# Softmax reciprocals spread over partitions by transfers inside SBUF, and normalization two pairs sooner, in an attention and feed-forward kernel

## The chip, the cores and the metric

One core of a Trainium2 chip runs the whole program. The metric is the device time of one execution in microseconds (us), the median of several runs. PE is the TensorE matmul, PEld its weight load, DVE VectorE, ACT ScalarE, POOL GpSimd, SP SyncE, which here only issues transfers (DMAs).

## What is computed

There are 2 batches of 12 heads, 448 tokens each, 64 numbers per head. After the attention come two feed-forward blocks, the second gated and with an RMS norm.

```
scores = cap * tanh(q @ k.T / sqrt(64) / cap)
attn   = exp(scores - max) / (sum + 1e-9);  x = attn @ v          # 896 x 768 over all heads
h = x @ w_in;   x = (h * sigmoid(1.702 h)) @ w_out                # 768 -> 2048 -> 768
xn = x / rms(x) * g;  out = (silu(xn @ w_gate) * (xn @ w_val)) @ w_out2   # 768 -> 1536 -> 768
```

The change concerns `attn / sum`: each head's output is multiplied by the reciprocal of its row sum, one number per token, which has to stand on all 64 partitions of the head.

## The kernel before, in words

**Pairs.** Attention works on 12 pairs of heads (`NPR` = 12). Pair p has its 2 x 64 output numbers on the 128 partitions and 448 tokens along the free dimension. The loop runs p from 0 to 12; iteration p makes the scores, tanh and exp of pair p and the output products, row sums and reciprocal of pair p-1. The instructions of every engine run in the order in which the program writes them (`manual_schedule`), so each engine is a queue: an instruction that waits holds all that is behind it. SP's and ACT's DMA issues stand in the same queues.

**One iteration from p = 3 on, by engine.** PE: `scores(p, 1)`, `scores(p, 2)` (L246), `scores_last(p)` (L255), `outputs(p-1)` (L294), `sums(p-1)` (L332), `scores(p+1, 0)`. ACT: four tanh (L275) and two exp (L278: `pa`, then `pb`). DVE: perhaps a normalization, `split_kq(p+2)` (L226, L227), `add_two(p)` (L314, needs the exp of `pa`), `copy_out(p-1)` (L306), the reciprocal of `sums(p-1)` (L337). POOL: `add_third(p)` (L319), which DVE does for the last pair. `sums(p-1)` needs the result of `add_third(p-1)`.

**PSUM.** The pool `ps_v` has two banks and three users in an iteration, in this order: `scores_last(p)`, `outputs(p-1)`, `sums(p-1)`. So `outputs(p)` gets the bank that `sums(p-1)` used and cannot start until the reciprocal of pair p-1 has read it. Likewise `scores_last(p+1)` waits for `copy_out(p-1)`.

**Reciprocals.** The reciprocal `rs` is a tile of 128 x 224: four groups of 32 equal rows, for two heads e and two halves j of the tokens. For pairs 0 to 8, `keep_recips` (L342) writes four rows to DRAM, and `spread` (L347), two iterations later, reads them back over all partitions into `r`. For pairs 9 to 11, four small matmuls (`spread_product`, L353) with a selection matrix `sel` do it, into PSUM.

**Normalization** of a pair is `norm_mul` (L368, L371 or L375, DVE), `norm_hi` (L380 on DVE for p < 8, L382 on ACT from p = 8 on) and `norm_lo` (L387, DVE). Pairs 0 to 4 are normalized five iterations after their scores (`norm(p-5)`), pairs 5 to 7 at the end of an iteration four later, pairs 8 to 10 in iteration 12, pair 11 inside the first feed-forward.

**Weights** come as units of 768 KB. A unit is loaded into one of three `raw` buffers (L112), decoded by ACT and DVE (`scale`, `shift`, `top`, `low`, then `high_part` on ACT, L156, and `low_part` on DVE, L161) and used by three matmuls for each block (`group`, L567 to L569). Units 0 to 2 are decoded partly during attention, by a `plan` of places: (4, "b") is place b of iteration 4, for example. Units 2 and 3 are finished while the first two columns of the feed-forward run. A column is 18 matmuls: two columns over tokens 0 to 383, four over tokens 384 to 895, and so on; the third column is the first that reads pair 11.

Of the kernel before, what the change touches and what calls it, by code (L numbers as in the profile page):

```python
# [17 lines left out]
def attn_moe_kernel(  # L18
# [36 lines left out]
    tiny = keep.tile([128, 1], F32, name="tiny")  # L55
    blk = keep.tile([128, 128], F32, name="blk")
    ones = keep.tile([128, 128], F32R, name="ones")
    sel = keep.tile([128, 64], F32, name="sel")
    gcol = keep.tile([128, KD], F32, name="gcol")
    xA = [keep.tile([128, KD, NT], F32R, name=f"x{i}") for i in range(2)]  # L60
    CUT = 384
# [45 lines left out]
    def load_to(u):  # L107
        while nload[0] <= min(u, len(units) - 1):
            w = nload[0]
            t = pools['raw'].tile([128, 6, 128, 2], U32, tag="raw", name="raw")  # L110
            for b0, n, s in units[w]:
                nc.sync.dma_start(out=t[:, b0:b0 + n].rearrange("p k f t -> p k (f t)"), in_=s)  # L112
            raw_t[w] = t
            nload[0] += 1
# [27 lines left out]
    def low(w):  # L142
        d, lo, hi = dec_t[w]
        nc.vector.scalar_tensor_tensor(  # L144
            out=d, in0=lo, scalar=29, in1=d, op0=ALU.logical_shift_right, op1=ALU.bitwise_or
        )
        if w != 2:
            load_to(w + 3)

    def high_part(w):  # L150
# [24 lines left out]
    def attention():  # L175
        with ExitStack() as actx:
# [9 lines left out]
            def constants():  # L186
                for e in range(2):
                    nc.gpsimd.memset(blk[half[e], half[e]], 1.0)
                    nc.gpsimd.memset(blk[half[e], half[1 - e]], 0.0)
                nc.gpsimd.memset(sel, 0.0)  # L190
                for n in range(4):
                    nc.gpsimd.memset(sel[32 * n:32 * n + 1], 1.0)

            xs, raws, vs, pa, pb, zt, nr, ts_ = {}, {}, {}, {}, {}, {}, {}, {}

# [85 lines left out]
                return pa[p][:, c] if c < 2 else pb[p][:, 0:2]  # L281

            opened = {}
            late = {}

            def outputs(p, cs=range(NC + 1)):
                if 0 in cs:
                    opened[p] = ps_v.tile([128, 512], F32, tag="v", name="v")
                ps = opened[p]
                for c in cs:  # L290
                    for n in range(4):
                        e, d0 = n // 2, n % 2 * 32
                        w = vs[p][:, e * NC + c if c < NC else 2 * NC + e]
                        nc.tensor.matmul(  # L294
                            out=ps[32 * n:32 * n + 32, 0:S], lhsT=w[:, d0:d0 + 32],
                            rhs=probs(p, c)[:, e] if c < NC else pb[p][:, 2],
                            start=(c == 0), stop=(c == NC), skip_group_check=True,
                        )
# [22 lines left out]
            def sums(p):  # L321
                ps = ps_v.tile([128, 512], F32, tag="v", name="v")
                streams = [ts_[p], *([pb[p][:, 0:2]] if p < THREE else []), None]
                for n, some in enumerate(streams):
                    for e in range(2):
                        for j in range(2):
                            if some is None:
                                w, t = blk[:, 64 * e:64 * e + 32], pb[p][:, 2]
                            else:
                                w, t = f(ones)[:, 0:32], some[:, e]  # L330
                            r0 = 64 * e + 32 * j
                            nc.tensor.matmul(  # L332
                                out=ps[r0:r0 + 32, 0:SH], lhsT=w, rhs=t[:, j * SH:(j + 1) * SH],
                                start=(n == 0), stop=some is None, skip_group_check=True,
                            )
                nr[p] = zrp.tile([128, SH], F32, tag="rs", name="rs", bufs=4)
                nc.vector.reciprocal(out=nr[p], in_=ps[:, 0:SH])  # L337

            def keep_recips(p):
                rs = nr[p]  # L340
                nr[p] = dram.tile([4, SH], F32, tag="recs", name="recs", bufs=3)
                nc.sync.dma_start(out=nr[p], in_=rs[0:128:32])  # L342

            def spread(p):
                d = nr[p].rearrange("(e j) n -> e (j n)", j=2)
                nr[p] = zrp.tile([128, S], F32, tag="r", name="r", bufs=3)
                nc.sync.dma_start(out=nr[p], in_=d.unsqueeze(1).to_broadcast([2, 64, S]))  # L347

            def spread_product(p, banks):
                for j in range(2):  # L350
                    for e in range(2):
                        quarter = slice(64 * e + 32 * j, 64 * e + 32 * j + 32)
                        nc.tensor.matmul(  # L353
                            out=banks[j][half[e]], lhsT=sel[quarter], rhs=nr[p][quarter],
                            start=True, stop=True, skip_group_check=True,
                        )
                nr[p] = banks

            def spread_late(p):
                if not late:  # L360
                    ps_s.tile([128, 2, 512], F32, tag="s", name="none")
                late[p] = ps_s.tile([128, 2, 512], F32, tag="s", name="late")[:, :, 0:SH]
                spread_product(p, [late[p][:, j] for j in range(2)])

            def norm_mul(p):
                r = nr.pop(p)
                if p < NPR - 3:
                    nc.vector.tensor_tensor(out=zt[p], in0=zt[p], in1=r, op=ALU.mult)  # L368
                elif p < NPR - 1:
                    zz = zt[p].rearrange("p (j n) -> p j n", j=2)  # L370
                    nc.vector.tensor_tensor(out=zz, in0=zz, in1=late[p], op=ALU.mult)  # L371
                else:
                    for j in range(2):
                        zz = zt[p][:, j * SH:(j + 1) * SH]
                        nc.vector.tensor_tensor(out=zz, in0=zz, in1=r[j], op=ALU.mult)  # L375

            def norm_hi(p):
                b, pp = divmod(p, NP)
# [12 lines left out]
            def norm(p):  # L391
                for step in (norm_mul, norm_hi, norm_lo):
                    step(p)
# [33 lines left out]
            scale_by_cap()  # L427

            EARLY = 3

            def products(p):
                outputs(p, range(NC + 1) if p else (2, NC))
                if p + 1 >= NPR - 1:
                    spread_late(p - 1)
                decode(p + 1, "a")
                if p < NPR - 1:
                    copy_out(p, "D")
                sums(p)

            for p in range(NPR + 1):  # L440
                load_kq(p + 3)
                load_v(p + 2)
                if 0 < p < 3:
                    load_to(p)
                if p == 0:
                    scores(0, 0)
                    tanh(0, 0)
# [28 lines left out]
                        exp(pa[p])  # L476
                    exp(pb[p])
                if 3 <= p < NPR:
                    spread(p - 3)
                if 5 <= p < NPR - 2:  # L480
                    norm(p - 5)
                decode(p, "b")
                if p + 2 < NPR:
                    split_kq(p + 2)
# [1 line left out]
                if p < NPR:  # L486
                    add_two(p)
                    decode(p, "d")
                if p == NPR:
                    norm_mul(p - 4)  # L490
                if p >= EARLY:
                    products(p - 1)
                    scores(p + 1, 0)
                if 1 <= p < NPR - 2:
                    keep_recips(p - 1)
                if p < NPR:
                    add_third(p)
                if p == NPR - 1:
                    norm_mul(p - 2)
                if NPR - 3 <= p < NPR:  # L500
                    norm(p - 4)
                if p == NPR:
                    copy_out(p - 1, "A")
                    some = (p - 3, p - 2, p - 4)
                    norm_mul(p - 2)
                    for step in (norm_hi, norm_lo):
                        for q_ in some:
                            step(q_)
            return spread_product, norm_mul, norm_hi, norm_lo

    def rest(spread_product, norm_mul, norm_hi, norm_lo):
        with ExitStack() as fctx:
            pools["ring1"] = fctx.enter_context(tc.tile_pool(name="ring1", bufs=3, reuse_waits="tile"))
            bigp = fctx.enter_context(tc.tile_pool(name="big", bufs=1, reuse_waits="tile"))
# [3 lines left out]
            def bank():  # L518
                return ps.tile([128, 512], F32, tag="b", name="b")
# [63 lines left out]
            def later(*fns):  # L583
                at(1, *[("D", True, fn) for fn in fns])
# [27 lines left out]
            for c in range(NC1):  # L612
# [9 lines left out]
                if c == 0:  # L622
# [2 lines left out]
                        + [(op, 3) for op in DVE_OPS] + [(op, 4) for op in ACT_OPS] + slots[0]  # L625
                    )
                    slots[0] = []
                if c == 0:
                    q3 = NPR - 1
                for n, (i, b) in enumerate(order):  # L630
                    last = ()
                    if c == 0 and n == 0:
                        later(lambda: spread_product(q3, [bank()[:, 0:B * S // 4] for _ in range(2)]))
                        later(lambda: norm_mul(q3), lambda: norm_hi(q3), lambda: run(shift, 2), lambda: norm_lo(q3))
                        last = (
                            lambda: [run(*some) for some in first], lambda: load_to(5), load_g,
                        )
                    ffn1(gA, u0 + i, i, b, slots[n], last)
# [247 lines left out]
```

## Time and profile before

| | |
|---|---|
| median of 3 runs | 589.24 us (588.69 to 590.09) |
| the profiled execution: its time, its span | 589.35 us, 587.5 us |
| PE, PEld, DVE, ACT, POOL busy | 99%, 83%, 71%, 47%, 10% |
| granted TensorE clock | 1.00 in nearly all of the span |
| start of the first feed-forward column | 91.19 us |

The span runs from the first to the last profiled instruction; the remaining 1.85 us lie around it. Times of rows count from the start of the span. A row "x16" of the timeline is 16 merged instructions. In brackets stands the idle time of the engine before it and what ended that.

### The profile page before, as it was taken

How to read it: one execution, taken by the hardware profiler on the slowest of the kernel's cores; microseconds unless marked ns; L12 is line 12 of the kernel's file. 1: busy time of each engine (PE TensorE's matmuls, PEld its weight loads, DVE VectorE, ACT ScalarE, POOL GpSimd, SP SyncE). 2: the span in 40 equal slices, each digit the busy share in tenths (PEclk: the TensorE clock that was granted, in tenths of full speed). 3: DMA queues.
4: the chain of work that ended last, by engine and by line, in shares of the span. 5: the costliest groups of instructions: out<-in, count | busy, mean ns of one | idle time of the engine just before them, and what ended most of it. 6: DMA issues, size and time to landing. Idle time of an engine off the chain costs nothing.

```text
span 587.5 us, 8371 instructions
## 1 busy us (share of the span) xinstructions
PE 581.6 (99%) x3390; PEld 487.6 (83%) x3390; DVE 418.5 (71%) x542; ACT 276.6 (47%) x371; POOL 59.2 (10%) x49
## 2 busy tenths in 40 slices
PE   9999999999999999999999999999999999999997
PEld 4455547898988889898999898989898998989887
DVE  4899987966736336566687999883587894678742
ACT  6999984754433335454444434443233331233300
POOL 0022320000000000000213012100122100222000
PEclk9999999999999999999999999999999999999999
DMA  8734510742443313333333333343133352133022
GB/s 285 268 125 149 158 50 6 211 162 101 152 126 107 108 54 108 108 107 108 108 108 108 108 108 113 121 152 99 54 109 109 108 189 80 55 107 108 1 89 98
DMA packets 55168, 67.91 MB, mean 116 GB/s; under 512 B 2998, under 2 KB 49882, under 8 KB 55130
## 3 DMA queue, kind: packets, MB, share of 16 engines
q1 hardware_dynamic: 54986, 67.15, 35.0%
q8 instruction: 26, 0.43, 0.3%
q10 hardware_dynamic: 144, 0.23, 0.1%
q14 instruction: 12, 0.10, 0.1%
HBM read 64.59 MB, written 2.78 MB: 115 GB/s over the span
## 4 chain that ended last, share of the span: by engine, by line
PE 97%; ACT 2%; issue 0%; DVE 0%
PE b L569 28%; PE b L568 28%; PE b L567 28%; PE v L294 6%; PE s L246 3%; PE v L332 2%; PE v L255 1%; ACT pa L275 1%; ACT pb L278 0%; ACT pb L275 0%; PE v L414 0%; ACT pa L278 0%; PE late L353 0%; PE b L709 0%; PE v L412 0%
## 5 line engine op out<-in xcount | busy, mean ns | idle before, releaser
L569 PE MATMUL b<-x,ring 128*128 128x384 f32 (+1 forms) x480 | 173.9, 362 | 0.0
L567 PE MATMUL b<-x,ring 128*128 128x384 f32 (+1 forms) x480 | 173.8, 362 | 0.0
L568 PE MATMUL b<-x,ring 128*128 128x384 f32 (+1 forms) x480 | 173.8, 362 | 0.0
L567 PEld LDWEIGHTS b<-x,ring 128*128 128x128 f32 x480 | 90.1, 188 | 10.2 <-DVE x L387 0.7
L568 PEld LDWEIGHTS b<-x,ring 128*128 128x128 f32 x480 | 90.1, 188 | 9.5
L569 PEld LDWEIGHTS b<-x,ring 128*128 128x128 f32 x480 | 90.1, 188 | 9.4
L161 DVE TENSOR_TENSOR ring<-dec,ring 128x768 fp32r<-128x768 f32 x68 | 77.2, 1136 | 28.1 <-ACT ring L156 28.1
L156 ACT ACTIVATE ring<-dec 128x768 fp32r<-128x768 f32 x67 | 56.1, 837 | 31.5 <-DVE dec L144 26.2
L569 PE MATMUL b<-g,ring 128*128 128x512 f32 (+1 forms) x192 | 69.7, 363 | 0.0
L568 PE MATMUL b<-g,ring 128*128 128x512 f32 (+1 forms) x192 | 69.6, 363 | 0.0
L567 PE MATMUL b<-g,ring 128*128 128x512 f32 (+1 forms) x192 | 69.5, 362 | 0.0
L144 DVE SCALAR_TENSOR_TENSOR dec<-raw,dec 128x768 uint32<-128x768 uint32 x68 | 66.9, 983 | 1.2
L138 DVE SCALAR_TENSOR_TENSOR dec<-raw,dec 128x768 uint32<-128x768 uint32 x68 | 64.8, 952 | 1.0
L130 ACT ACTIVATE dec<-raw 128x768 f32<-128x768 f32 x66 | 59.2, 897 | 5.0 <-issue 2.5
L569 PE MATMUL b<-uA,ring 128*128 128x512 f32 (+1 forms) x144 | 52.1, 362 | 0.0
L568 PE MATMUL b<-uA,ring 128*128 128x512 f32 (+1 forms) x144 | 52.1, 362 | 0.0
L567 PE MATMUL b<-uA,ring 128*128 128x512 f32 (+1 forms) x144 | 52.1, 362 | 0.0
L599 DVE TENSOR_TENSOR g<-gg,g 128x384 fp32r<-128x384 f32 (+1 forms) x32 | 20.0, 624 | 40.6 <-ACT g L596 40.6
L741 POOL TENSOR_TENSOR a<-a,gg 128x512 f32<-128x512 f32 (+1 forms) x18 | 29.2, 1622 | 187.1 <-DVE gg L734 179.9
L744 ACT ACTIVATE uA<-a 128x512 fp32r<-128x512 f32 (+1 forms) x24 | 13.9, 580 | 70.4 <-POOL a L741 52.1
L134 DVE TENSOR_SCALAR dec<-dec 128x768 uint32<-128x768 uint32 x68 | 39.4, 579 | 0.0
L568 PEld LDWEIGHTS b<-g,ring 128*128 128x128 f32 x192 | 36.0, 188 | 3.9
(93 smaller groups left out, 670.9 us busy)
## 6 DMA issues: line engine op xcount, KB each, us to landing
raw<-in_moe_w_out SPq DMA_DIRECT2D x20, 768.0 KB
raw<-in_moe_w_in SPq DMA_DIRECT2D x16, 768.0 KB
raw<-in_moe_w_gate SPq DMA_DIRECT2D x12, 768.0 KB
raw<-in_moe_w_val SPq DMA_DIRECT2D x12, 768.0 KB
raw<-in_moe_w_out SPq DMA_DIRECT2D x8, 512.0 KB
v<-in_v SPq DMA_DIRECT2D x12, 256.0 KB
kq<-in_k SPq DMA_DIRECT2D x11, 256.0 KB
kq<-in_q SPq DMA_DIRECT2D x11, 224.0 KB
```

Of the source, the lines that this page charges most:

```text
L130: nc.scalar.activation(out=f(d), in_=f(hi), func=AF.Copy, scale=2.0 ** -112)
L134: nc.vector.tensor_scalar(out=d, in0=d, scalar1=3, scalar2=None, op0=ALU.logical_shift_left)
L138: nc.vector.scalar_tensor_tensor(out=d, in0=hi, scalar=0x80000000, in1=d, op0=ALU.bitwise_and, op1=ALU.bitwise_or)
L144: nc.vector.scalar_tensor_tensor(out=d, in0=lo, scalar=29, in1=d, op0=ALU.logical_shift_right, op1=ALU.bitwise_or)
L156: nc.scalar.activation(out=t[:, 0], in_=f(dec_t[w][0]), func=AF.Copy)
L161: nc.vector.tensor_tensor(out=t[:, 1], in0=f(d), in1=f(t[:, 0]), op=ALU.subtract)
L294: nc.tensor.matmul(out=ps[32 * n:32 * n + 32, 0:S], lhsT=w[:, d0:d0 + 32], rhs=probs(p, c)[:, e] if c < NC else pb[p][:, 2], start=(c == 0 ...
L567: nc.tensor.matmul(out=wide(o, b), lhsT=w0, rhs=x0, start=first, stop=False)
L568: nc.tensor.matmul(out=wide(o, b), lhsT=w0, rhs=x1, start=False, stop=False)
L569: nc.tensor.matmul(out=wide(o, b), lhsT=w1, rhs=x0, start=False, stop=last)
L599: nc.vector.tensor_tensor(out=gA[1].at(i, hb), in0=gg[0], in1=f(gA[0].at(i, hb)), op=ALU.subtract)
L741: eng.tensor_tensor(out=t[0], in0=t[0], in1=t[1], op=ALU.mult)
```

## The change

- All 12 pairs use the same `spread(p)`: four DMAs from SBUF to SBUF, each of 64 rows of 224 numbers, from one half j of `rs` to every second partition of `r`. The sums are put at other partitions for that (`r0`). The DMAs are issued from SP directly behind the reciprocal, in the iteration after the pair's scores; for the last pair, two of the four are issued from ACT.
- `keep_recips`, `spread_product`, `spread_late`, the matrix `sel` and its five memsets go.
- `norm(p-3)` takes the place of `norm(p-5)`, from iteration 3 to 11; pair 9 is normalized at the end of iteration 11, pair 10 in iteration 12, pair 11 in the feed-forward with `shift(2)` and `top(2)` ahead of it.
- `outputs(11)` writes to a bank of `ps_s` in place of `ps_v`.
- Weight units 1 to 4 are loaded at the starts of iterations 3, 5, 7 and 9; before, units 1 to 3 were issued in iteration 1 and unit 4 after `low(1)` in iteration 7.

```diff
-        if w != 2:
+        if w > 2:
             load_to(w + 3)
...
             def outputs(p, cs=range(NC + 1)):
                 if 0 in cs:
-                    opened[p] = ps_v.tile([128, 512], F32, tag="v", name="v")
+                    if p < NPR - 1:
+                        opened[p] = ps_v.tile([128, 512], F32, tag="v", name="v")
+                    else:
+                        ps_s.tile([128, 2, 512], F32, tag="s", name="none")
+                        opened[p] = ps_s.tile([128, 2, 512], F32, tag="s", name="s")[:, 0]
...
-                            r0 = 64 * e + 32 * j
+                            r0 = 64 * j + 32 * e
...
+            def spread(p):
                 rs = nr[p]
                 nr[p] = zrp.tile([128, S], F32, tag="r", name="r", bufs=3)
-                nc.sync.dma_start(out=nr[p], in_=d.unsqueeze(1).to_broadcast([2, 64, S]))
...
                 for j in range(2):
+                    for i in range(2):
+                        eng = nc.scalar if j and p == NPR - 1 else nc.sync
+                        eng.dma_start(out=nr[p][i:128:2, j * SH:(j + 1) * SH], in_=rs[64 * j:64 * j + 64])
...
             def norm_mul(p):
+                nc.vector.tensor_tensor(out=zt[p], in0=zt[p], in1=nr.pop(p), op=ALU.mult)
...
+            RAW = {3: 1, 5: 2, 7: 3, 9: 4}
             def products(p):
                 outputs(p, range(NC + 1) if p else (2, NC))
-                if p + 1 >= NPR - 1:
-                    spread_late(p - 1)
...
-                if 0 < p < 3:
-                    load_to(p)
+                if p in RAW:
+                    load_to(RAW[p])
...
                 if 3 <= p < NPR:
-                    spread(p - 3)
-                if 5 <= p < NPR - 2:
-                    norm(p - 5)
+                    norm(p - 3)
                 decode(p, "b")
...
-                if p == NPR:
-                    norm_mul(p - 4)
                 if p >= EARLY:
                     products(p - 1)
                     scores(p + 1, 0)
-                if 1 <= p < NPR - 2:
-                    keep_recips(p - 1)
+                if p >= 1:
+                    spread(p - 1)
                 if p < NPR:
                     add_third(p)
                 if p == NPR - 1:
-                    norm_mul(p - 2)
-                if NPR - 3 <= p < NPR:
-                    norm(p - 4)
+                    norm(p - 2)
                 if p == NPR:
                     copy_out(p - 1, "A")
-                    some = (p - 3, p - 2, p - 4)
-                    norm_mul(p - 2)
-                    for step in (norm_hi, norm_lo):
-                        for q_ in some:
-                            step(q_)
+                    norm(p - 2)
...
-                        later(lambda: spread_product(q3, [bank()[:, 0:B * S // 4] for _ in range(2)]))
-                        later(lambda: norm_mul(q3), lambda: norm_hi(q3), lambda: run(shift, 2), lambda: norm_lo(q3))
+                        later(lambda: run(shift, 2), lambda: run(top, 2), *norm_last)
```

## Rows read from the trace of the kernel before

**Rows 1.** The page's first part: busy us, share, instructions of each engine.

```profile
PE 581.6 (99%) x3390; PEld 487.6 (83%) x3390; DVE 418.5 (71%) x542; ACT 276.6 (47%) x371; POOL 59.2 (10%) x49
```

**Rows 2.** Stretches: length, busy us of PE, PEld, DVE, ACT, POOL; clock, DMA share, GB/s.

```profile
34.00:61.00 27.00, 27.00 (x296) 13.99 (x295) 26.00 (x33) 24.98 (x25) 7.86 (x5) 1.00 0.49 151
...
76.00:81.00 5.00, 5.00 (x62) 2.77 (x58) 4.40 (x6) 4.64 (x5) 1.50 (x1) 1.00 0.13 48
...
102.00:331.00 229.00, 229.00 (x1135) 205.36 (x1134) 147.63 (x192) 107.28 (x166) 11.68 (x10) 1.00 0.37 118
```

**Rows 3.** Timeline: start, length, engine, line; reciprocals and output products.

```profile
32.25 1.55 DVE L337 RECIPROCAL rs<-v 128x224 f32<-128x224 f32 x1
...
33.90 1.71 PE L294 MATMUL v<-pa,v 128*32 128x448 f32 x16 [0.31 <-ACT pa L275]
...
39.11 1.56 DVE L337 RECIPROCAL rs<-v 128x224 f32<-128x224 f32 x1
...
40.77 1.71 PE L294 MATMUL v<-pa,v 128*32 128x448 f32 x16
...
45.54 1.55 DVE L337 RECIPROCAL rs<-v 128x224 f32<-128x224 f32 x1
...
81.66 1.69 PE L294 MATMUL v<-pa,v 128*32 128x448 f32 x16
```

**Rows 4.** Timeline: the matmuls that spread reciprocals, and PE beside the last.

```profile
84.78 0.61 PE L353 MATMUL late<-rs,sel 32*64 32x224 f32 x8
...
94.28 0.34 PE L569 MATMUL b<-x,ring 128*128 128x384 f32 x1
...
95.08 0.44 PE L567 MATMUL b<-x,ring 128*128 128x384 f32 x1
```

**Rows 5.** Timeline of DVE: normalizations.

```profile
40.57 0.86 DVE L368 TENSOR_TENSOR z<-z,r 128x448 f32<-128x448 f32 x1
...
75.07 0.63 DVE L368 TENSOR_TENSOR z<-z,r 128x448 f32<-128x448 f32 x1 [0.42 <-DMA r<-recs]
...
76.70 0.95 DVE L161 TENSOR_TENSOR ring<-dec,ring 128x768 fp32r<-128x768 f32 x1
```

**Rows 6.** Timeline of DVE in iteration 3.

```profile
27.91 0.59 DVE L226 CAST x<-kq 128x832 fp32r<-128x832 f32 x1 [0.43 <-DMA kq<-in_q]
...
30.71 1.09 DVE L314 TENSOR_TENSOR ts<-pa 128x896 f32<-128x896 f32 x1 [0.28 <-ACT pa L278]
```

**Rows 7.** Timeline of iterations 11 and 12.

```profile
84.66 1.43 ACT L278 ACTIVATE pb<-pb,capt 128x1344 f32<-128x1344 f32 x1
...
84.89 1.09 DVE L314 TENSOR_TENSOR ts<-pa 128x896 f32<-128x896 f32 x1 [1.70 <-ACT pa L278]
...
87.90 1.03 DVE L319 TENSOR_TENSOR ts<-ts,pb 128x896 f32<-128x896 f32 x1
...
90.30 0.59 PE L332 MATMUL v<-ts,ones 128*32 128x224 f32 x8
...
96.05 0.58 ACT L382 ACTIVATE x<-z 128x448 fp32r<-128x448 f32 x1 [1.41 <-DVE z L375]
```

**Rows 8.** Timeline: one small load, its issue and its first use.

```profile
1.20 0.41 SPq L400 DMA_DIRECT2D capt<-in_cap  x1
...
4.18 0.16 DVE L219 RECIPROCAL tsc<-capt 128x1 f32<-128x1 f32 x1 [2.70 <-DMA capt<-in_cap]
```

**Rows 9.** Timeline of the first feed-forward: decoding on DVE, and PE.

```profile
101.77 0.39 PE L567 MATMUL b<-x,ring 128*128 128x512 f32 x1
...
102.35 0.96 DVE L161 TENSOR_TENSOR ring<-dec,ring 128x768 fp32r<-128x768 f32 x1 [0.91 <-ACT ring L156]
...
108.89 0.95 DVE L161 TENSOR_TENSOR ring<-dec,ring 128x768 fp32r<-128x768 f32 x1
...
111.06 0.39 PE L569 MATMUL b<-x,ring 128*128 128x512 f32 x1
```

**Rows 10.** A stretch behind the last matmuls, columns as above.

```profile
584.00:586.00 2.00, 0.09 (x1) 0.00 (x0) 0.56 (x1) 0.00 (x0) 0.00 (x0) 1.00 0.49 185
```

More of the change, by code (lines that the diff above doesn't have):

```diff
@@ L57, in attn_moe_kernel @@
     ones = keep.tile([128, 128], F32R, name="ones")
-    sel = keep.tile([128, 64], F32, name="sel")
     gcol = keep.tile([128, KD], F32, name="gcol")
@@ L189, in constants @@
                     nc.gpsimd.memset(blk[half[e], half[1 - e]], 0.0)
-                nc.gpsimd.memset(sel, 0.0)
-                for n in range(4):
-                    nc.gpsimd.memset(sel[32 * n:32 * n + 1], 1.0)
             xs, raws, vs, pa, pb, zt, nr, ts_ = {}, {}, {}, {}, {}, {}, {}, {}
@@ L283, in attention @@
             opened = {}
-            late = {}
             def outputs(p, cs=range(NC + 1)):
                 if 0 in cs:
-                    opened[p] = ps_v.tile([128, 512], F32, tag="v", name="v")
+                    if p < NPR - 1:
[3 more added lines that the diff above has]
+                        opened[p] = ps_s.tile([128, 2, 512], F32, tag="s", name="s")[:, 0]
                 ps = opened[p]
@@ L337, in sums @@
                 nc.vector.reciprocal(out=nr[p], in_=ps[:, 0:SH])
-            def keep_recips(p):
+            def spread(p):
                 rs = nr[p]
[L341 to L345, printed above, removed]
                 nr[p] = zrp.tile([128, S], F32, tag="r", name="r", bufs=3)
-                nc.sync.dma_start(out=nr[p], in_=d.unsqueeze(1).to_broadcast([2, 64, S]))
-            def spread_product(p, banks):
                 for j in range(2):
[L351 to L363, printed above, removed]
-            def norm_mul(p):
[L366 to L375, printed above, removed]
+                    for i in range(2):
+                        eng = nc.scalar if j and p == NPR - 1 else nc.sync
+                        eng.dma_start(out=nr[p][i:128:2, j * SH:(j + 1) * SH], in_=rs[64 * j:64 * j + 64])
+            def norm_mul(p):
+                nc.vector.tensor_tensor(out=zt[p], in0=zt[p], in1=nr.pop(p), op=ALU.mult)
             def norm_hi(p):
@@ L498, in attention, with rest @@
                 if p == NPR - 1:
-                    norm_mul(p - 2)
-                if NPR - 3 <= p < NPR:
-                    norm(p - 4)
+                    norm(p - 2)
                 if p == NPR:
                     copy_out(p - 1, "A")
-                    some = (p - 3, p - 2, p - 4)
-                    norm_mul(p - 2)
-                    for step in (norm_hi, norm_lo):
-                        for q_ in some:
-                            step(q_)
-            return spread_product, norm_mul, norm_hi, norm_lo
-    def rest(spread_product, norm_mul, norm_hi, norm_lo):
+                    norm(p - 2)
+            return lambda: norm_mul(NPR - 1), lambda: norm_hi(NPR - 1), lambda: norm_lo(NPR - 1)
+    def rest(*norm_last):
         with ExitStack() as fctx:
@@ L627, in rest @@
                     slots[0] = []
-                if c == 0:
-                    q3 = NPR - 1
                 for n, (i, b) in enumerate(order):
```

## The prediction, made before the changed kernel had run

> **What bounds the kernel now.** I read the page's first part, then the stretches, then the timeline of the attention stage engine by engine.
>
> The page says that PE is busy 99% of the span [rows 1]. In the feed-forward this is nearly the whole story: from 102 to 331 us PE is busy 229.00 of 229.00 us, DVE 147.63 [rows 2]. There a shift of the start of the stage shifts the end by as much, and DVE work costs nothing unless it comes late.
>
> In attention it is half the story. From 34 to 61 us PE is busy 27.00 of 27.00 us, but DVE 26.00 and ACT 24.98 [rows 2]: three engines run at nearly the same pace. Which one leads is seen in the timeline. The reciprocal of pair 2 ends at 32.25 + 1.55 = 33.80, and the output products of pair 3 start at 33.90; that of pair 3 ends at 39.11 + 1.56 = 40.67, and the next output products start at 40.77 [rows 3]. This is the PSUM bank: `outputs(p)` takes the bank that the reciprocal of pair p-1 reads. The trace names ACT as the releaser of 33.90, but the reciprocal ends 0.1 before each of them, and the order of the bank's users asks for it. So in these iterations DVE's queue sets PE's pace, although PE's share is higher. What is put into DVE's queue here goes straight into the time.
>
> **The change part by part.** The sum is made against the profiled execution, 589.35 us with a span of 587.5; the median is 589.24, so nothing has to be rescaled.
>
> *Removed from PE.* The three spreads by matmul take 0.61 us each [rows 4]. The third stands alone in the first feed-forward: matmuls of 384 columns start 0.17 apart there (from 101.77 to 111.06 lie 41 of 512 columns [rows 9], 0.227 each, of which three quarters), the one before it started at 94.28 and the one behind it at 95.08 [rows 4], so it costs 95.08 - 94.28 - 0.17 = 0.63 us. The first two stand ahead of `sums(10)` and `sums(11)`; whether they count depends on what `sums(11)` waits for, below.
>
> *Added to DVE in iterations 3 and 4.* Normalization starts in iteration 3 and not 5. Its total is the same, but iterations 3 and 4 get one more, and these hold the decoding of units 0 and 1. One normalization takes 76.70 - 75.07 = 1.63 us in the queue (the next instruction starts then), and 0.86 - 0.63 = 0.23 more when its product runs beside POOL: 1.86 [rows 5].
>
> Iteration 3: DVE is idle 0.43 us ahead of `split_kq`, and 0.28 ahead of `add_two` [rows 6]. `norm(0)` starts in the first gap, at 27.48, and the split behind it at 29.11 in place of 27.91: 1.20 late. The wait of 0.28 vanishes, and `add_two` and the reciprocal of pair 2 come 0.92 late. PE stood waiting for that reciprocal, so `outputs(3)` is 0.92 late.
>
> Iteration 4: from 33.80 to 40.67 DVE has no gap, so `norm(1)` adds its whole 1.86. The reciprocal of pair 3 ends at 40.67 + 0.92 + 1.86 = 43.45, and `outputs(4)` is 2.78 late.
>
> From iteration 5 on DVE does what it did before. One of its iterations without decoding is 45.54 + 1.55 - 40.67 = 6.42 us [rows 3]. From `outputs(4)` to `outputs(10)` PE takes 81.66 - 40.77 = 40.89, 6.82 for each of six [rows 3]. The late PE is no longer paced by DVE except where `low(1)` adds to it in iteration 7; at some 6.7 us each, an estimate between the 6.42 and the 6.82, it regains 0.6. `outputs(10)` then starts at 81.66 + 2.78 - 0.6 = 83.84: 2.2 late.
>
> *Added wait in iteration 11.* This edit looks free and is not. `norm(8)` now stands ahead of `add_two(11)` on DVE. For pairs from 8 on, `norm_hi` runs on ACT, and ACT's queue has all tanh and exp of pair 11 ahead of it. `norm_lo(8)` on DVE waits for `norm_hi(8)`, and behind it wait `add_two(11)`, `copy_out(10)`, the reciprocal of pair 10 and `add_third(11)`, which is DVE's for this pair; `sums(11)` on PE waits for that last one. Now `add_two(11)` starts at 84.89, when the exp of `pa` ends; the exp of `pb` ends at 84.66 + 1.43 = 86.09 [rows 7]. ACT is as late as PE that feeds it, 2.2 us: `pb` ends at 88.29. Then come `norm_hi(8)` (0.58, as the ACT row of its line [rows 7]; say to 88.8), `norm_lo(8)` (0.55 of the queue) and what stands from `add_two(11)` to the end of `add_third(11)`, 87.90 + 1.03 - 84.89 = 4.04 [rows 7]: 93.4. `sums(11)` starts at 93.45, now at 90.30 [rows 7]: 3.15 late. PE has nothing else: with `outputs(11)` done at about 91.1 it stands still for some 2.3 us. In this idle time the gain of the first two spreads (1.2 us) and of the free bank for `outputs(11)` is lost.
>
> *The last pair's reciprocals by DMA.* The reciprocal of pair 11 ends some 2.3 us after the first feed-forward matmul: `norm(9)` is ahead of it on DVE. Two issues on each of two queues follow, at 0.41 each or a little more [rows 8]: 1.0. ACT's two stand ahead of `copy_out(11)` and `norm_hi(10)`, so `norm_lo(10)` waits for them too. The landing is not in the trace. Nearest from below: a small load was issued by 1.61 and used at 4.18, 2.57 later [rows 8]. From above: today's spread moves 224 KB at 48 GB/s, with 0.13 of 16 engines busy [rows 2], which is 4.8 us. I take 2.6, since each transfer is small. Then the data is there 5.9 us in, before DVE has done `norm_lo(10)`, `shift(2)` and `top(2)`, which I put at 6.4. `norm_lo(11)` ends 8.2 in. PE reads pair 11 now at 101.77 [rows 9], that is 10.58 after 91.19, and 9.95 without the third spread. So the DMA itself is hidden, with 1.7 to spare; at 4.8 this is gone.
>
> A rule of the Trainium skill bears on the landing. The trace shows a spread on two engines' worth of bandwidth [rows 2]. "DMA: Bandwidth & Descriptors", section "Why a DMA increments its semaphore by 16 and not by 1", says that the slowest dimension of the access pattern sets how many engines a transfer uses: two for today's pattern, with which the trace agrees, sixteen for rows of 64. By it the landing would lie near the lower bound, and the sum stays; by the same page's "Rules for kernel authors" small transfers pay mostly overhead, so four are no better than one.
>
> *Behind it, the decoding of unit 3.* `norm_hi(11)` ends now at 96.63, 5.4 after the first matmul [rows 7], then 7.6: 2.2 later. ACT's first Silu and `low(2)` follow it; `top(2)`, 1 us, is already done. So the chain of decoding is about 1.1 later. From 102.35 to 109.84 it has next to no gap [rows 9]. Its end, the low part of unit 3, is needed at 111.06, a slack of 1.22 [rows 9], of which the missing third spread takes 0.63. 1.1 + 0.63 - 1.22 = 0.5 us of PE waiting. Bounds: 0, and 2.2 with a landing of 4.8.
>
> *At nothing.* The five memsets on POOL lie at the start, where nobody waits for them. The other `r0` sends the same matmuls to other partitions. Loading units later takes SP's block in iteration 1 away; each unit now has an iteration before its decoding. The four issues hold SP's queue 2 us and the next pair's loads with it, but those are due a whole iteration later. If that cover were gone, `split_kq` would wait, again on DVE.
>
> Sum: 589.35 + 3.15 - 0.63 + 0.5 = **592.4 us**.
>
> **The rivals.**
>
> *A. Faster: DVE's load stays off PE's path.* If the bank did not tie `outputs` to the reciprocal, only the removed matmuls would count: 589.35 - 0.61 - 0.61 - 0.63 = 587.5. For it: PE's share, and PE named for nearly everything by it [rows 1, 2]. Against: the 0.1 us between reciprocal and output products, each time [rows 3]. It decides if DVE's iteration 4 ends before 41 us in spite of one more normalization.
>
> *B. One of the two.* Only iterations 3 and 4 reach PE: 2.2 late, less two spreads, less the third, gives 589.35 + 2.2 - 1.22 - 0.63 = 589.7. Only iteration 11 does: `add_third(11)` ends at 86.09 + 5.1 = 91.2, `sums(11)` 0.95 late, and 589.35 + 0.95 - 0.63 + 0.5 = 590.2. Either is within 0.2% (1.2 us), about what a measurement of this kernel can tell from no change.
>
> *C. The spread lands late.* At 4.8 us, `norm_mul(11)` starts 8.1 in and not 6.4: 1.7 on the decoding, 594.1.
>
> *D. The clock falls in the new idle time.* After the last matmuls the granted clock is still 1.00 through two idle microseconds [rows 10]; the new stop is of some 2.3, with another near 2 in iteration 4. If it falls to 1.2 GHz, each microsecond at that level loses half of its work: 2 to 6 us cost 1 to 3, so 593.4 to 595.4. This is the rule of the Trainium skill that speaks against the change: "TensorE: Matmul & The Clock Gate", section "Part 1: The HAM clock gate", says that an idle TensorE falls to half its clock. The rows show no fall within 2 us.
>
> **How the numbers follow.** Chances: forecast 0.60, A 0.13, B 0.16, C 0.05, D 0.06. The forecast's own range is 591.2 to 593.8: the regained 0.6 could be 0 to 1, the decoding 0 to 1.2, and the chain of iteration 11 may be 0.5 off. The range that leaves out A and half of D, and of B only what lies below 589, is 588.9 to 594.5. Faster by over 0.2%: A, 0.13, and 0.01 for B at its edge, 0.14. Within 0.2%: B and the forecast's lowest edge, 0.16. Slower: 0.70.
>
> **What would show it.** In the profile after: reciprocals of pairs 2 and 3 that end near 34.7 and 43.5, with `outputs(4)` right behind; `norm_lo(8)` on DVE waiting for ACT, and `sums(11)` for DVE, near 88.8 and 93.4; no L353; the first feed-forward matmul at 94.3; a short wait of PE near 113.5 for the low part of unit 3. The prediction is wrong if PE passes iteration 4 without a gap, if DVE passes `norm_lo(8)` before `pb` is done, or if `norm_mul(11)` waits for its DMA.

## The result, and the profile after

| | before | after |
|---|---|---|
| time, median of 4 (us) | 589.34 (588.69 to 590.09) | 597.37 (597.18 to 597.63) |
| ratio, 95% interval | | 1.0136 [1.0119, 1.0154] |
| span of the profiled execution (us) | 587.5 | 595.4 |
| its mean granted clock | 1.00 | 0.994 |

The changed kernel is slower, as forecast, but by 8.0 us and not by 3. The time lies outside the range.

First the page of the kernel after: busy time of each engine, the granted clock in 40 slices, and the chain that ended last.

```profile
PE 581.1 (98%) x3366; PEld 488.2 (82%) x3366; DVE 418.5 (70%) x541; ACT 277.1 (47%) x371; POOL 58.4 (10%) x44
...
PEclk9999997999999999999999999999999999999999
...
PE 94%; DVE 2%; ACT 1%; issue 1%; DMA 1%; SPq 1%; ACTq 0%; DVEq 0%
```

Against [rows 1], no engine's busy time grew by more than 0.6 us, and PE's fell by 0.5. What grew is idle time, and one digit of the clock, in the slice from 89 to 104 us, is 7 and not 9. So I looked at that stretch alone, in windows (length, busy us of PE, PEld, DVE, ACT, POOL, clock, DMA share, GB/s):

```profile
90.00:91.00 1.00, 0.47 (x8) 0.00 (x0) 1.00 (x3) 0.00 (x0) 0.00 (x0) 1.00 0.00 0
91.00:92.00 1.00, 0.00 (x0) 0.00 (x0) 1.00 (x2) 0.00 (x0) 0.00 (x0) 1.00 0.00 0
...
95.00:96.00 1.00, 0.00 (x0) 0.00 (x0) 1.00 (x1) 0.00 (x0) 0.00 (x0) 0.56 0.24 57
96.00:97.00 1.00, 0.00 (x0) 0.00 (x0) 0.73 (x2) 0.00 (x0) 0.00 (x0) 0.50 0.00 0
97.00:98.00 1.00, 0.00 (x0) 0.00 (x0) 0.00 (x0) 0.28 (x1) 0.00 (x0) 0.50 0.51 108
...
100.00:101.00 1.00, 1.00 (x4) 1.00 (x4) 1.00 (x2) 0.00 (x0) 0.00 (x0) 0.50 0.00 0
101.00:102.00 1.00, 1.00 (x5) 1.00 (x5) 0.38 (x1) 0.58 (x1) 0.00 (x0) 0.52 0.00 0
102.00:103.00 1.00, 1.00 (x7) 1.00 (x7) 0.63 (x1) 0.99 (x1) 0.00 (x0) 1.00 0.00 0
```

PE stands still twice, and from 95.1 to 102 it has half its clock. While DVE fills the first stop, in the second one nearly nothing runs: from 97 to 98, of the engines, only ACT, for 0.28 us. The timeline of the same stretch names both waits:

```profile
32.98 1.55 DVE L336 RECIPROCAL rs<-v 128x224 f32<-128x224 f32 x1
...
34.63 1.71 PE L293 MATMUL v<-pa,v 128*32 128x448 f32 x16 [0.55 <-issue]
...
41.33 1.55 DVE L336 RECIPROCAL rs<-v 128x224 f32<-128x224 f32 x1
...
42.98 1.71 PE L293 MATMUL v<-pa,v 128*32 128x448 f32 x16 [0.55 <-issue]
...
83.52 1.69 PE L293 MATMUL v<-pa,v 128*32 128x448 f32 x16
...
87.80 0.59 ACT L354 ACTIVATE x<-z 128x448 fp32r<-128x448 f32 x1
88.42 0.63 DVE L359 TENSOR_TENSOR x<-z,x 128x448 fp32r<-128x448 f32 x1 [4.49 <-ACT x L354]
...
93.14 0.58 PE L331 MATMUL v<-ts,ones 128*32 128x224 f32 x8 [2.67 <-DVE ts L318]
...
94.71 1.55 DVE L336 RECIPROCAL rs<-v 128x224 f32<-128x224 f32 x1
...
96.29 1.38 ACTq L344 DMA_DIRECT2D r<-rs  x2
97.72 0.55 ACT L303 ACTIVATE z<-s 128x448 f32<-128x448 f32 x1 [2.79 <-DVE z L347]
98.32 0.69 PE L528 MATMUL b<-x,ring 128*128 128x384 f32 x1 [4.21 <-ACT z L303]
98.80 0.52 PE L529 MATMUL b<-x,ring 128*128 128x384 f32 x1
...
101.99 0.34 PE L530 MATMUL b<-x,ring 128*128 128x384 f32 x1
102.16 0.34 PE L528 MATMUL b<-x,ring 128*128 128x384 f32 x1
102.33 0.33 PE L529 MATMUL b<-x,ring 128*128 128x384 f32 x1
```

The first stop is the predicted one: DVE waits at `norm_lo(8)` (L359) for `norm_hi(8)` on ACT (L354), and `sums(11)` (L331) starts at 93.14; the forecast was 93.45. The second was not predicted. The first feed-forward matmul waits 4.21 us for `copy_out(11)` on ACT (L303). The feed-forward's first accumulator lies in the PSUM bank that holds `outputs(11)` (both are in bank 0 of the built program), so it can't be written before that bank is copied. And `copy_out(11)` stands on ACT behind two DMA issues (L344), which wait for the reciprocal of pair 11, done at 94.71 + 1.55 = 96.26. For ACT's row the trace names DVE's L347; the two issues directly ahead of it, 96.29 to 97.67, are what it stood behind.

The 8 us then add up. The first feed-forward matmul starts at 98.32, 7.13 after the 91.19 of before. From 98.32 to 102.16 twelve matmuls take 3.84 us, and at the full clock's spacing of 0.173 (102.16 to 102.33, and so on) 2.08: 1.76 lost to the clock. The third spread matmul is gone: -0.63. That is +8.26, and the span grew by 7.9. Most of the 0.36 between them is in the kernel before: its first three feed-forward matmuls, from 91.19 to 91.84, took 0.65 and not 0.52, and the one behind the third spread lasted 0.1 longer than its neighbours [rows 4].

### The profile page after: what moved, and what is told of

Read it like the earlier page. It is cut to its first block, busy times and chain, and to the rows that moved or that the text cites. A ratio compares the mean times of both kernels' runs of the same rounds, so it can differ in the third digit from the quotient of the medians.

```text
span 595.4 us, 8361 instructions
## 1 busy us (share of the span) xinstructions
PE 581.1 (98%) x3366; PEld 488.2 (82%) x3366; DVE 418.5 (70%) x541; ACT 277.1 (47%) x371; POOL 58.4 (10%) x44
## 4 chain that ended last, share of the span: by engine, by line
PE 94%; DVE 2%; ACT 1%; issue 1%; DMA 1%; SPq 1%; ACTq 0%; DVEq 0%
PE b L529 28%; PE b L528 28%; PE b L530 28%; PE v L293 4%; PE s L242 3%; PE v L331 1%; PE v L251 1%; DMA r<-rs 1%; SPq L344 1%; DVE ts L313 1%; DVE rs L336 1%; PE s L293 1%; PE v L386 0%; ACT pa L274 0%; ACT pa L271 0%
```

## The experiments

The theory after the result has three causes: the wait for ACT at `norm_lo(8)` (2.5 us), the bank with the clock that falls in it (4 to 5 us), and normalization in iterations 3 and 4 (2 us). Its rivals: the spread's landing is late, ACT's two DMA issues alone are the cause, or the clock alone. Each run has the kernel before beside it, with a median of 589.25 to 589.36.

**e1: another bank for the last output products.** Against the changed kernel; the write of one column takes the place of the tile that nothing uses.

```
-                        ps_s.tile([128, 2, 512], F32, tag="s", name="none")
...
+                if p == NPR - 1:
+                    hold = ps_s.tile([128, 2, 512], F32, tag="s", name="hold")
+                    nc.vector.memset(hold[:, 0, 0:1], 0.0)
```

> The changed kernel with the output products of pair 11 in another PSUM bank: a small memset in iteration 11 occupies bank 0, so the products take bank 4, which the feed-forward needs five columns later. Theory (the 4.2 us ahead of the first feed-forward matmul are a wait for copy_out(11), which reads bank 0 and stands on ACT behind two DMA issues that wait for the last reciprocal): the wait goes, the first feed-forward matmul comes near 94.2 instead of 98.3, and with only 2.7 us of stop left the clock stays at 1.00, which saves another 1.6: about 591.5 us. Rival (the feed-forward waits for the normalization or for the DMAs of the last pairs, and the bank is only what the profile names): no change, 597.4, or the wait comes back in the third column. Rival for the clock alone: the stop of 2.7 us is enough to let the clock fall, 593.

592.92 us (592.33 to 594.17), ratio 1.0062 [1.0047, 1.0077]: 4.45 us of the 8.0 are gone. The timeline and the waits (total, times, longest us) of this kernel:

```profile
93.25 0.59 PE L330 MATMUL v<-ts,ones 128*32 128x224 f32 x8 [2.79 <-DVE ts L317]
93.63 0.59 PE L330 MATMUL v<-pb,blk 128*32 128x224 f32 x8
94.14 0.44 PE L530 MATMUL b<-x,ring 128*128 128x384 f32 x1
```

```profile
PE v L330 <- DVE ts L317: 2.8, 1, 2.8
PE b L532 <- DVE ring L160: 1.0, 1, 1.0
```

The feed-forward starts at 94.14, with no wait, where the prediction had 94.3. So this kernel is the one that the prediction described, and its time is 0.5 above the predicted 592.4. The rivals of this run, that the feed-forward waits for the normalization or for the last pair's DMAs, fall with it. The first stop is still there, and in the profiled execution the clock held 1.00 through it. In the other three executions the mean clock was 0.994, 0.997 and 0.999, and the one at 0.994 took 594.17, while the one at 0.997 took 592.33, no longer than the rest. So with a stop of 2.8 us some executions show a lower clock, and one of them a longer time; only the first was profiled, so where the clock fell in the others isn't seen. The second wait is the predicted one for unit 3's low part, 1.0 and not 0.5; in the changed kernel PE was too late to meet it.

**e2: the last pair's spread on SP alone.** `eng = nc.sync` in all four issues.

> The changed kernel with all four DMAs of the last pair issued from SP, none from ACT; the bank stays as it is. Theory (copy_out(11) waits behind the DMA issues on ACT): copy_out(11) runs behind the decoding scale(2) near 95 instead of 97.7, the first feed-forward matmul near 95.5; if the clock does not fall, 592.8, and if the now shorter second stop still lets it fall, 594.4. The last pair's data lands about 1 us later, which stays hidden. Rival (the wait is for the landing of the reciprocals): the first matmul comes 1 us later than in the changed kernel, 598.4.

594.21 us, ratio 1.0080 [1.0063, 1.0097]. PE's waits in the stretch behind 88 us:

```profile
PE v L331 <- DVE ts L318: 2.7, 1, 2.7
PE b L528 <- ACT z L303: 1.3, 1, 1.3
```

The bank is shared as in the changed kernel, and with ACT's issues gone the wait shrinks from 4.2 to 1.3: bank and issues make the stop together. The first feed-forward matmul comes at 95.41, as the theory had it (95.5), and the time is its case with a fallen clock (594.4). The clock is lower in all four executions (0.994 to 0.997); in windows of the profiled one:

```profile
94.00:95.00 1.00, 0.11 (x4) 0.00 (x0) 0.83 (x2) 1.00 (x3) 0.00 (x0) 0.74 0.37 86
95.00:96.00 1.00, 0.59 (x2) 0.59 (x3) 1.00 (x1) 0.36 (x1) 0.00 (x0) 0.50 0.24 57
```

The last spread does land late here: `norm_mul(11)` waits 0.7 us for it, which PE doesn't see.

**e3: e1, and `norm_hi(8)` on DVE.** On top of e1's edit:

```
-                if p < NPR - 4:
+                if p < NPR - 3:
```

> As the one with the other bank, and norm_hi(8) on DVE instead of ACT, so that DVE does not wait for the exp of pair 11. Theory: the stop of 2.7 us ahead of sums(11) goes, sums(11) starts near 90.7 and the feed-forward near 91.7: 589.0 us if unit 3 is decoded in time, 589.6 if not. What is left against the kernel before is iteration 3 and 4 (about 2.1 us late), set against 1.2 + 0.6 us of matmuls removed. Rival (DVE's total work, not its wait for ACT, makes sums(11) late): add_third(11) ends less than 1 us sooner, 591.

590.43 us, ratio 1.0018 [1.0009, 1.0028]: 2.5 us less than e1. The wait ahead of `sums(11)` is 0.56, the feed-forward starts at 91.57, and the wait for unit 3 stays:

```profile
90.68 0.59 PE L330 MATMUL v<-ts,ones 128*32 128x224 f32 x8 [0.56 <-DVE ts L317]
...
111.81 0.50 PE L532 MATMUL b<-x,ring 128*128 128x512 f32 x1 [0.99 <-DVE ring L160]
```

All ten executions show a clock of 0.999 or 1.00. The theory had at most 589.6: it held for the feed-forward's start (91.7) and took too little for unit 3, whose wait is 1.0. The rival falls: `add_third(11)` ends 2.5 us sooner than in the changed kernel, at 90.53. What is left over the kernel before is 1.1 us.

**e4: spreads SBUF to SBUF, normalization when it was before.** The changed kernel with SP alone, one more buffer for the spread (4, not 3), and the old places of `norm` (from iteration 5 on).

> The changed kernel with the order of normalization of the kernel before (pairs 0 to 4 five iterations later, 5 to 7 four, 8 to 10 in iteration 12), four r buffers instead of three, and all DMAs from SP. The four transfers for all pairs, the loads and the bank stay as changed. Theory (the time is in DVE's queue, not in the transfers): outputs(4) is back at 40.8 and outputs(10) near 81.7, sums(11) starts near 89.0, the feed-forward near 90.0, so the two spreads by matmul show as a gain; then the last pair's data lands near 97.5, 7.5 us after the first feed-forward matmul, and the decoding behind it costs PE up to 1.7 us: 587.5 to 589.2. Rival (the transfers inside SBUF cost by contention or by holding SP's queue): later than 590.

589.93 us (589.44 to 592.08), ratio 1.0016 [1.0006, 1.0026]. Less was gained than expected, since a new wait appears, on DVE's timeline and SP's:

```profile
35.40 0.58 DVE L127 TENSOR_SCALAR dec<-raw 128x768 f32<-128x768 f32 x1 [1.82 <-DMA raw<-in_moe_w_in]
```

```profile
24.32 2.89 SPq L344 DMA_DIRECT2D r<-rs  x4
27.31 0.53 SPq L196 DMA_DIRECT2D kq<-in_k  x1
...
28.84 0.43 SPq L111 DMA_DIRECT2D raw<-in_moe_w_in  x1
```

Unit 1 is now loaded in iteration 3, behind four issues that hold SP for 2.89 us and behind the next pair's loads, and comes 1.82 us late for `scale(1)` in iteration 4. In the changed kernel `norm(0)` and `norm(1)` stand ahead of `scale(1)`, which starts at 36.28 and waits for nothing: one late thing hid the other. Two of the ten executions, at 591.75 and 592.08, have a mean clock of 0.996, the other eight 0.999 or 1.00; the profiled one, at 1.00, shows no wait of PE above 1.2 us behind 20 us, so why the clock fell in those two stays open.

**e5: e4, with unit 1 loaded in iteration 1.** `RAW = {1: 1, 5: 2, 7: 3, 9: 4}`.

> The late normalization once more, with weight unit 1 loaded at the start of iteration 1 instead of 3; units 2 to 4 stay spread. In that run DVE stood 1.82 us in iteration 4 for unit 1, whose load was issued in iteration 3 behind four spreads and three loads. Theory: that wait goes, outputs(10) comes near 81.7 instead of 82.65 and the feed-forward near 90.0 instead of 90.94; the decoding of unit 3 starts as much sooner, so PE's wait for it stays near 1.2: 588.9. Rival (the load is late because the transfers inside SBUF slow all others): DVE waits as long, 589.9.

588.45 us, ratio 0.9986 [0.9977, 0.9995]. DVE's wait is gone and the feed-forward starts at 89.53, 1.4 sooner than in e4 and 2.0 sooner than in e3. What PE still waits for, and `copy_out(11)` on ACT:

```profile
PE b L538 <- DVE ring L160: 1.3, 1, 1.3
PE v L331 <- DVE ts L318: 0.5, 1, 0.5
...
88.25 0.54 ACT L303 ACTIVATE z<-s 128x448 f32<-128x448 f32 x1 [1.77 <-PE s L293]
```

**e6: e5, with the decoding of unit 3 ahead of the last pair's low part.**

```
-                        later(lambda: run(shift, 2), lambda: run(top, 2), *norm_last)
+                        mul_, hi_, lo_ = norm_last
+                        later(lambda: run(shift, 2), lambda: run(top, 2), mul_, hi_, lambda: run(low, 2),
+                            lambda: run(high_part, 2), lo_, lambda: run(low_part, 2))
```

> As that one, and in the first feed-forward low(2) runs between norm_hi(11) and norm_lo(11), high_part(2) right behind norm_hi(11) on ACT, low_part(2) right behind norm_lo(11). Theory: DVE's waits for ACT (0.65, 1.74 and 0.91 us there) are filled, the low part of unit 3 is ready about 1.2 sooner, and PE's wait for it nearly goes: 587.6, below the kernel before by what the three spreads by matmul cost there, 1.2 + 0.6. Rival (ACT is the longer chain: the table load and the first Silu come later by high_part(2)): unit 3 is no sooner, 588.9 or more.

587.14 us (586.83 to 587.17), ratio 0.9964 [0.995, 0.9978]. The wait of 1.3 is gone:

```profile
PE v L331 <- DVE ts L318: 0.5, 1, 0.5
PE v L293 <- ACT pa L271: 0.3, 1, 0.3
PE v L293 <- issue: 0.2, 1, 0.2
```

This is the best version found: 2.1 us under the kernel before that ran beside it (589.25), 10.2 under the changed one. The three spreads by matmul are gone in it, and no wait of PE above 0.5 us is left in the stretch from 30 to 140 us.

**e7: the loads alone.** The kernel before with `if w > 2` and the changed kernel's `RAW`.

> The kernel before with the spread weight loads alone: units 1 to 4 in iterations 3, 5, 7 and 9. Theory: with one short transfer and not four ahead of it on SP, unit 1 lands before its decoding in iteration 4 needs it, or within 1 us of it: 589.0 to 590.0. Rival (spreading the loads costs by itself): DVE waits 1.8 us in iteration 4 and PE with it, 590.5 or more. Rival (it gains, since SP's 10 us block in iteration 1 goes): 588.5.

592.22 us, ratio 1.0050 [1.0036, 1.0063]. The slowdown came, but not from where any theory expected it. Unit 1 is in time; DVE waits for the spreads, by the waits of attention (20 to 101 us):

```profile
DVE z L368 <- DMA r<-recs: 7.2, 5, 2.3
```

Before, it is one wait, of 0.42 ([rows 5]). The loads, moved into the later iterations, meet the old spread through DRAM, which moves at 48 GB/s [rows 2], and it comes up to 2.3 us late for `norm_mul`. Its issue isn't late: SP issues the spread of pair 3 at 49.97 in this kernel, and `norm_mul(3)` waits for it until 62.42. So the time lies behind the issue, in the transfers; whether in their queue or in the DMA engines that they share, no run separates. With the changed kernel's spread SBUF to SBUF no such wait shows: `norm_mul` waits there for no DMA.

**e8: PE kept busy behind `sums(11)`.** The changed kernel with 20 added matmuls of 448 columns, whose results nothing uses.

> The changed kernel with 20 extra matmuls of 448 columns behind sums(11), into a bank that nobody reads; they fill the stop ahead of the feed-forward and change nothing in what is waited for. Theory (the clock falls because of the second stop, and its price is the 0.32 instead of 0.17 us between feed-forward matmuls for some 11 of them): the first feed-forward matmul still comes near 98.3, the clock stays at 1.00, 595.7. Rival (the clock falls for the stop ahead of sums(11) already, or for another reason): half clock as before, 597.4.

595.88 us (595.51 to 597.26), ratio 1.0118 [1.0104, 1.0132]. Windows of this kernel:

```profile
93.00:94.00 1.00, 1.00 (x14) 0.60 (x3) 0.51 (x1) 1.00 (x2) 0.00 (x0) 0.66 0.40 95
94.00:95.00 1.00, 1.00 (x4) 0.90 (x3) 1.00 (x2) 0.26 (x1) 0.00 (x0) 0.50 0.33 77
...
97.00:98.00 1.00, 1.00 (x6) 0.91 (x6) 0.00 (x0) 0.96 (x2) 0.00 (x0) 1.00 0.85 176
```

With PE busy from 92.5 on, the clock falls all the same, at 93.3, and is back before 97, while the added matmuls still run. The feed-forward starts at 99.09, 0.8 later than in the changed kernel because the added matmuls ran at half clock, and from its first matmul on it has the full spacing of 0.17: +0.77 for the start and -1.76 for the clock give -1.0, as the spans do (594.4 and 595.4). In two of the four executions the mean clock was 1.00, and these took 595.51 and 595.59, as the theory had it (595.7); the other two, at 0.997, took 596.17 and 597.26. So the first stop, 2.7 us, can be enough by itself, and need not be.

**e9: `norm_hi(8)` on DVE alone.** e3's second edit on the changed kernel, to see whether the second stop is enough by itself too.

> The changed kernel with one edit: the high part of pair 8 is rounded on VectorE, as that of the pairs before it, and no longer on ACT behind the exp of pair 11. The bank of the last output products stays as in the changed kernel. Both theories expect the first stop of TensorE, 2.67 us ahead of the last sums, to shrink to about 0.6, the last sums to start near 90.7 and not at 93.14, and the second stop, about 4.2 us for the copy of the last output products, to stay: the first feed-forward matmul near 95.8. Theory 1, the first stop is what lets the clock fall (it fell with TensorE kept busy behind that stop): the clock holds through a single stop of 4.2, the feed-forward's matmuls start 0.17 apart from the first on, and the time is 597.4 - 2.5 - 1.65 = 593.2. Theory 2, the long second stop alone is enough: the clock is at half near the first feed-forward matmuls, and the time is 594.9.

595.47 us (594.64 to 596.11), ratio 1.0099 [1.0082, 1.0116]. Its PE rows and windows:

```profile
90.90 0.58 PE L331 MATMUL v<-ts,ones 128*32 128x224 f32 x8 [0.46 <-DVE ts L318]
...
96.06 0.69 PE L528 MATMUL b<-x,ring 128*128 128x384 f32 x1 [4.20 <-ACT z L303]
...
102.28 0.34 PE L529 MATMUL b<-x,ring 128*128 128x384 f32 x1
```

```profile
94.00:95.00 1.00, 0.00 (x0) 0.00 (x0) 0.50 (x2) 0.00 (x0) 0.00 (x0) 1.00 0.00 0
95.00:96.00 1.00, 0.00 (x0) 0.00 (x0) 0.00 (x0) 0.53 (x2) 0.00 (x0) 0.70 0.71 152
...
101.00:102.00 1.00, 1.00 (x5) 1.00 (x5) 0.00 (x0) 0.04 (x1) 0.00 (x0) 0.50 0.00 0
```

Theory 2 held: one stop of 4.2 us lets the clock fall, in all four executions (0.994 to 0.997). Nineteen matmuls from 96.06 to 102.28 take 6.22 us and not 19 x 0.173 = 3.29: 2.9 lost. Against the profiled execution after, the start is 2.26 sooner and the loss 1.17 larger, so 1.1 less; the spans are 594.3 and 595.4. Of the 2.26 us that the removed wait gives, the clock takes back half in this execution. That holds for the two executions at 0.994 (596.06 and 596.11); the two at 0.997 took 594.64 and 594.88, which is what theory 2 had.

## Why the prediction was wrong

**Held: what DVE does to PE in iterations 3 and 4.** `outputs(3)` at 34.63 and `outputs(4)` at 42.98 stand right behind their reciprocals; forecast were about 34.8 and 43.5, against 33.90 and 40.77 [rows 3]. Of the 0.5 by which the second is sooner, 0.2 was gained in iteration 3, and 0.34 is `scale(1)`, which took 0.58 at 36.28 and not 0.92 as before: POOL's `add_third(3)`, which ran beside it then, had ended at 34.79. That this is the reason is argued from the rows, not tested. `outputs(10)` starts at 83.52 (forecast 83.84), 1.86 later than the 81.66 of before [rows 3]; the term said 2.2. In e5, with normalization put back and unit 1 loaded sooner, it starts at 81.23, against 83.16 in e3. Rival A falls with it.

**Held: the wait in iteration 11.** `norm_lo(8)` at 88.42 (forecast 88.8), `sums(11)` at 93.14 (93.45). Without the wait, e1 to e3, the time falls by 2.5. Rival B needed only one of the two mechanisms; both are there.

**Failed: "The last pair's reciprocals by DMA".** The step said that ACT's two issues stand ahead of `copy_out(11)`, and then asked only who waits for `norm_hi(10)`, which is queued behind it. It did not ask who waits for `copy_out(11)` itself, and the sum took the new bank of `outputs(11)` for free. The bank makes the first feed-forward column wait for it: 98.32 and not 94.3. The tied bank is the same rule as the one that the prediction read off the reciprocals [rows 3]; it was applied within attention and not across the border to the next stage, where the changed kernel's `outputs` uses another pool. e1 shows the price: 4.45 us together with the clock. This accounts for the miss: of the 5.0 us between 592.4 and 597.37, 4.0 is this start, 1.76 the clock, and -0.5 the wait for unit 3 that did not come (5.3 in all). In e5 and e6, with bank 0 shared as well, `copy_out(11)` runs on an idle ACT and the feed-forward does not wait, so there the shared bank costs nothing, as its copy can run at once. In the changed kernel too `outputs(11)` was done at 90.47 and ACT idle until 93.56; a copy placed there, ahead of `norm_hi(9)`, was not tried.

**Failed as a consequence: rival D, given 0.06.** The clock fell, which the sum left out. Its price in the changed kernel, 1.76, lies in the 1 to 3 given for it. The evidence against it, two idle microseconds at 1.00 [rows 10], was true and too short for a stop forecast at 2.3: 2.7 to 2.8 us went with a lower clock in some executions (e1, e8), 2.7 and then 1.3 in all four (e2), 4.2 in all four (e9). Which of the two stops let it fall in the changed kernel isn't shown. "TensorE: Matmul & The Clock Gate", section "Part 1: The HAM clock gate", of the Trainium skill says that an idle TensorE falls to half its clock; the rows of e9 agree, 1.00 until 95 and 0.50 from 96 on.

**Mis-sized: unit 3.** 1.0 us in e1 and e3, not 0.5, inside the bounds of 0 and 2.2. In the changed kernel PE is 4 us later and does not wait for it.

**Wrong, and hidden: "At nothing".** "Each unit now has an iteration before its decoding" does not hold for unit 1: e4 shows it 1.82 us late once the normalizations are out of its way. The four issues took 2.4 to 3.2 us of SP (SP's rows in the kernel after), not 2.

**Held: the landing is hidden.** The page's row of DMA issues after gives it 2.0 us (2.6 was taken):

```profile
r<-rs SPq DMA_DIRECT2D x46, 56.0 KB, 2.0
```

`norm_mul(11)` starts at 100.77, behind DVE's own queue, with no wait for its DMA, and none in e1, where PE is not late. Rival C falls.

The steps on the way from the changed kernel to e6: another bank 4.45 (597.37 to 592.92), `norm_hi(8)` 2.5 (to 590.43), normalization as before with unit 1 loaded in time 2.0 (e5, to 588.45; e5 is not built on e3, and keeps the shared bank, SP alone and `norm_hi(8)` on ACT), the order of decoding 1.3 (to 587.14). So the changed kernel's spreads, with other work ordered around them, stand in a kernel 2.1 us under the one before. Of the 10.2, 8.9 lie in the order of work, the bank and the issuing queue that came with them, and 1.3 in an order of decoding that is new in e6.

## What to carry to other kernels

Where an edit puts a waiting instruction on a queue, follow every instruction behind it to its reader, and follow each PSUM bank past the end of the stage to the next stage's first accumulator. A stop of PE can cost more than its length: 1.76 us on top of 4.21 here. So one as long as those here, 2.7 us and more, should be priced with the matmuls behind it at half speed as a case of its own. An edit that looks free in the trace may be covered by another cost of the same change: take that cost out and look again, as in e4.

## What was not expected of the hardware

- The clock fell for a stop of 2.69 us with 20 matmuls directly behind it (e8, 0.50 from 94 on), and held 1.00 for one of 2.79 in e1's profiled execution. With no wait above 1.3 us no execution of e3, e5 or e6 was under 0.999, but two of ten of e4 were at 0.996. What decides stays open.
- In the profiled executions the half clock began at 95.1 in the kernel after, 1 us into the second stop, and at 95.4 in e9, 3.5 us into its only long one. It ended at 102.0 and 102.2, though PE had begun again at 98.32 and at 96.06: starting sooner gave 7 more matmuls at half speed and no sooner return. The executions of e9 at 0.997, which have no trace, had less of it.
- Four SBUF-to-SBUF issues in a row held SP for 2.38 (kernel after) to 3.63 us (e5), 0.6 to 0.9 each, where one small load's issue took 0.41 [rows 8].
